# Score maxima in two parts: banks of their own for each, and moved steps, in pooled attention with two expert layers

## The chip, the cores and the metric

One Trainium2 chip, one of its cores. The metric is the device time of one execution in microseconds, median of the runs shown.

## The reference

```python
# attention: B=4, H=8, S=1152, D=64, query rows pooled in twos
q_pool = q.reshape(B, H, S // 2, 2, D).mean(axis=3)
scores = np.matmul(q_pool, k.transpose(0, 1, 3, 2)) / np.sqrt(D)
scores = scores - np.max(scores, axis=-1, keepdims=True)
attn = np.exp(scores)
attn = attn / (np.sum(attn, axis=-1, keepdims=True) + 1e-09)
x = np.matmul(attn, v)                    # then (2304, 512) = tokens x features
# soft mixture: logits over 32 slots, softmax over tokens (dispatch) and over slots (combine)
logits = x @ phi
d = softmax(logits, axis=0); slot_input = d.T @ x
slot_out[e] = np.maximum(slot_input[e] @ w1[e], 0) @ w2[e]     # 8 experts of 4 slots, width 1024
x = softmax(logits, axis=1) @ slot_out
# second layer: each token goes to its best expert by cosine with expert_emb / tau
out[mask] = gate_w[mask, None] * (np.maximum(x[mask] @ w1[e], 0) @ w2[e])
```

## The kernel before

All is float32. The work on the attention goes by pairs of heads: 16 pairs, four for each of the four batches, and 18 steps for each pair (`step`, L663; n counts all steps, i the pair, s the step in it). A step of pair i computes scores of one block of 128 keys against one half of the 576 pooled query rows, for the two heads: per head two matmuls into one bank (`scores`, L366; the second, L375, adds the low part of the query and, by a row of ones, the negated maximum) and an Exp on ScalarE into a `pt` tile (L376). Steps 0 to 8 are the first half of the queries, 9 to 17 the second. The weighted sums with V (`weighted`, L425) of a half are done at one go, at step 10 for the first and at step 1 of the next pair for the second (`VISITS`), 36 matmul instructions at L433; behind the second the sums of the weights go through matmuls with ones (`weight_sums`, L402, first at L410), whose input `acc` is added up by GpSimd (`add_up`, L379: L389, L391, L397) from `pt` and from a partial sum `part` by VectorE (L394, steps 9 and 18, which is step 0 of the next pair).

The maxima have to be known before the scores. For the pair ahead they are found in nine pieces (j = 0 to 8) of 64 query rows for each of two heads: `s_max` (L322) multiplies 128 rows with the 1152 keys, three matmuls of 384 columns into the three banks of a tile `s` (L334), and VectorE reduces the tile (L343) to one negated maximum a row, in column j of `nm`. There is one such tile (pool `ps_s`, one buffer of three banks; the other five banks are the ring `ps_e`, `new_e`, `new_t`). In the first pair some maxima are found "apart", in three banks of the ring, by three reductions and a joining one (L340, L341). `n_group` (L346) transposes `nm` for pieces 0 to 4 (`n0`, step 12) or 5 to 8 (`n1`, step 3 of the pair itself), and two small DMAs put it into `ql` (L354).

The order is written out by hand, in tables from step to action (L34 to L53): `MAXS` the pieces of the maximum, `SIDE` the other work on TensorE (q0, q1: transposing pooled queries; n0, n1; r: reciprocals of the sums; x0 to x2: normalised rows and logits), `FIRST` and `FMAX` the same for pair 0, `BATCH` the work at a batch's end. `keys_ahead` (L647) follows `TURN`, `HIGH` and `REST`: a third of the keys of pair i+2 is transposed by VectorE (L278), copied rounded by ScalarE (L281), and the remainder is formed by GpSimd (L285). Keys are loaded into one buffer `kn` by four DMAs at step 15 (`KLOAD`, L246, for pair i+3); `HEADS` says when a third of the keys is copied by head into `u` by DMAs from SP's queue (L291, L292), `LOADW` when a quarter of a weight tile is loaded (L588). In one step the order of issue is: scores, maximum, side work, batch work, weighted sums, the rests of side and batch work (on VectorE and ScalarE), `add_up` for the step before, `keys_ahead`, `q_by_heads`, `by_heads`, key load, query load, V load, weight piece. Every engine, and SP's queue of DMAs, takes its instructions in this order.

At a batch's end, in the second pair after it, `max_group` (L502; table value 18, so step 0) transposes the logits of 576 rows into the first bank of an `s` tile, VectorE takes the maximum over them (L508) and joins it with that of earlier batches (L510), and ScalarE's Exp reads the bank (L512). `d_group` (19, step 1) transposes the result, `sl_group` (21, step 3) multiplies it with the rows. The last batch's groups follow the loop (L714 on), and then the two expert layers, whose weights come from HBM by loads at L127.

Of the kernel before, what the change touches and what calls it, by code (L numbers as in the profile page):

```python
# [8 lines left out]
F32 = mybir.dt.float32  # L9
F32R = mybir.dt.float32r  # L10
I32 = mybir.dt.int32
AF = mybir.ActivationFunctionType
ALU = mybir.AluOpType
AX = mybir.AxisListType
PSUM = bass.MemoryType.PSUM
ET = mybir.EngineType
P = 128
# [14 lines left out]


SIDE = {5: 'q1', 7: 'r', 9: 'x0', 1: 'q0', 13: 'x2', 12: 'n0', 3: 'n1', 14: 'x1'}  # L34
MAXS = {2: 0, 4: 1, 6: 2, 8: 3, 10: 4, 16: 7, 1: 8, 14: 6, 11: 5}
BATCH = {18: 'm', 19: 'd', 21: 's'}

TURN = {2: 0, 9: 2, 12: 1}
FTURN = {9: 1, 11: 0, 10: 2}
HIGH = {16: 2, 13: 1, 11: 0}  # L40
REST = {17: 0, 8: 1, 10: 2}
HEADS = (11, 15, 17)
QHEADS = 6
VISITS = (10, 19)

# [2 lines left out]
FQHEADS = 14  # L48

PREAT = 2  # L50
LOADW = (3, 6, 10)
QLOAD, KLOAD, VLOAD, QSUM = 5, 15, 6, 12
FQLOAD, FQSUM = 12, 17  # L53

# [2 lines left out]
def kernel(  # L57
# [14 lines left out]
    nc = tc.nc  # L72
    B, H, S, D = q.shape
# [3 lines left out]
    J = PQ // 64  # L77
    JB = J // 2
    NPAIR = H // 2
    KC = S // 3  # L80
# [14 lines left out]
    ident = const.tile([P, P], F32, name="ident")  # L95
# [43 lines left out]
    apart = const.tile([P, P // NS, NS], F32, name="apart")  # L139
# [27 lines left out]
    smax = [keep.tile([P, 1], F32, name=f"smax{b}") for b in range(B)]  # L167
# [4 lines left out]
    sm = att.enter_context(tc.tile_pool(name="sm", bufs=4))  # L172
    xp = att.enter_context(tc.tile_pool(name="xp", bufs=1))
# [8 lines left out]
    pairs = [{"b": i // NPAIR, "hp": i % NPAIR} for i in range(NPT)]  # L182
    xb = [{} for _ in range(B)]
# [24 lines left out]
    kh = [khl.tile([P, S], F32R, name=f"kh{i}") for i in range(2)]  # L208
    qb = [khl.tile([P, n, P], F32R, name=f"qb{g}") for g, n in enumerate((6, J - 6))]
# [8 lines left out]
    ps_s = att.enter_context(tc.tile_pool(name="ps_s", bufs=1, space=PSUM))  # L218
# [50 lines left out]
    def new_e():  # L269
        return ps_e.tile([P, 512], F32, tag="e", name="e")  # L270

    def new_t():
        return new_e()


    def turn(i, g):
        t = pairs[i]["kl", g] = khl.tile([P, KC], F32R, tag=f"kl{g}", name=f"kl{g}", bufs=2)
        nc.vector.transpose(out=t.bitcast(F32), in_=pairs[i]["kn"][:, 12 * g : 12 * g + 12].rearrange("p n d -> p (n d)"))  # L278
# [8 lines left out]
    def by_heads(i, g):  # L287
        cs = slice(g * KC, (g + 1) * KC)
        for h in range(2):
            hi, lo = kh[i % 2][own[h], cs].bitcast(F32), pairs[i]["kl", g][own[h]].bitcast(F32)  # L290
            nc.sync.dma_start(out=uw[g][0:64, :, h].bitcast(F32), in_=hi.unsqueeze(1).to_broadcast([64, 2, KC]))  # L291
            nc.sync.dma_start(out=us[g][64:128, h].bitcast(F32), in_=lo)  # L292
# [21 lines left out]
    def q_by_heads(i, cs=None):  # L314
        _, qh, ql = sets[i % 2]
        cs = cs or slice(0, PQ)
        for h in range(2):
            for dst, src in ((qh[0:64], hq), (qh[64:128], hq), (ql[0:64], lq)):
                nc.sync.dma_start(out=dst[:, h, cs].bitcast(F32), in_=src[own[h], cs].bitcast(F32))


    def s_max(i, j, apart=False):  # L322
        p = pairs[i]
        if j in (0, 5):
            p["nm", j] = sm.tile([P, 5], F32, tag="nm", name="nm", bufs=3)
        j0 = 5 if j > 4 else 0
        nm = p["nm", j0][:, j - j0 : j - j0 + 1]
        if apart:
            ss = [new_e()[:, 0:KC] for _ in range(3)]
        else:  # L330
            s = ps_s.tile([P, 3, 512], F32, tag="s", name="s")
            ss = [s[:, c, 0:KC] for c in range(3)]
        for c in range(3):
            nc.tensor.matmul(  # L334
                ss[c], qb[j // 6][:, j % 6, :], kh[i % 2][:, c * KC : (c + 1) * KC], start=True, stop=True
            )
        if apart:
            n3 = sm.tile([P, 3], F32, tag="n3", name="n3", bufs=2)
            for c in range(3):
                nc.vector.tensor_reduce(out=n3[:, c : c + 1], in_=ss[c], axis=AX.X, op=ALU.max, negate=True)  # L340
            nc.vector.tensor_reduce(out=nm, in_=n3, axis=AX.X, op=ALU.min)  # L341
        else:
            nc.vector.tensor_reduce(out=nm, in_=s[:, :, 0:KC], axis=AX.XY, op=ALU.max, negate=True)  # L343


    def n_group(i, part):  # L346
        j0, n = (5, J - 5) if part else (0, 5)
        t = new_t()
        nc.tensor.transpose(t[0:n, 0:P], pairs[i]["nm", j0][:, 0:n], ident)
        nr = sm.tile([5, P], F32R, tag="nr", name="nr", bufs=2)  # L350
        nc.scalar.activation(out=nr[0:n], in_=t[0:n, 0:P], func=AF.Copy)
        ql = sets[i % 2][2]
        for h in range(2):
            nc.sync.dma_start(  # L354
                out=ql[64:65, h, j0 * 64 : (j0 + n) * 64].rearrange("o (j q) -> o j q", q=64).bitcast(F32),
                in_=nr[0:n, own[h]].bitcast(F32),
            )
        yield
# [141 lines left out]


    def max_group(b):  # L502
        t = ps_s.tile([P, 3, 512], F32, tag="s", name="s")[:, 0, :]
        nc.tensor.transpose(t[:, 0:P], lk[:, b * JB : (b + 1) * JB, :].rearrange("p m n -> p (m n)"), ident)
        n = P + 64
        nc.tensor.transpose(t[:, P:n], xb[b]["l4"].rearrange("p m n -> p (m n)"), ident[0:64, 0:64])
        yield
        nc.vector.tensor_reduce(out=smax[b], in_=t[:, 0:n], axis=AX.X, op=ALU.max, negate=True)  # L508
        if b:
            nc.vector.tensor_tensor(out=smax[b], in0=smax[b], in1=smax[b - 1], op=ALU.min)  # L510
        dt = xb[b]["dt"] = xp.tile([P, P + 64], F32, tag="dt", name="dt")
        nc.scalar.activation(out=dt, in_=t[:, 0 : P + 64], func=AF.Exp, bias=smax[b])  # L512
        if b:
            cor = xb[b]["cor"] = sm.tile([P, 1], F32, tag="cor", name="cor", bufs=1)
            nc.scalar.activation(out=cor, in_=smax[b - 1], func=AF.Exp, scale=-1.0, bias=smax[b])
# [27 lines left out]
    def slot_sums(b, t):  # L543
        x, xr, d = (xb[b][n] for n in ("x", "xr", "d"))
        for m in range(JB):
            ms = slice(m * NS, (m + 1) * NS)
            nc.tensor.matmul(t[ms], d[:, 0, ms], x[:, m, :], start=True, stop=False, tile_position=(0, m * NS))
        for m in range(JB):
            ms, cs = slice(m * NS, (m + 1) * NS), slice(m * P, (m + 1) * P)
            nc.tensor.matmul(t[ms, cs], d[0:64, 1, ms], xr[:, cs], start=False, stop=True, tile_position=(0, m * NS))  # L550

    def sl_group(b):
        t = ps_s.tile([P, 3, 512], F32, tag="s", name="s")[:, 0, :] if b == B - 1 else new_t()
        slot_sums(b, t)
        yield
        if b == B - 1:
            new = xb[b]["new"] = xp.tile([P, DM], F32, tag="new", name="new")
            nc.scalar.activation(out=new, in_=t, func=AF.Copy)
        elif b:
            nc.vector.scalar_tensor_tensor(  # L560
                out=slots, in0=slots, scalar=xb[b]["cor"], in1=t, op0=ALU.mult, op1=ALU.add
            )
        else:
            nc.vector.tensor_copy(slots, t)
# [60 lines left out]
    for h in range(2):  # L625
        nc.sync.dma_start(
            out=ip[own[h], :, P + h * NS : P + (h + 1) * NS], in_=phi.rearrange("(c p) n -> p c n", p=P)[own[h]]
# [5 lines left out]
    def begin(live, g):  # L633
        live.append(g)
        next(g, None)
# [11 lines left out]
    def keys_ahead(i, s):  # L647
        if i + 2 < NPT:
            if s in (TURN if i else FTURN):
                turn(i + 2, (TURN if i else FTURN)[s])  # L650
            if s in HIGH:
# [11 lines left out]
    def step(n):  # L663
        i, s = divmod(n, NCH)
        live = []
        if n < NST:
            for h in range(2):
                scores(n, h)
            early = i == 0
            if s in (FMAX if early else MAXS):  # L670
                j = (FMAX if early else MAXS)[s]
                at = i + 1 - (s < 6 and j > 4)
# [4 lines left out]
            for late in range(2):  # L677
                at, s1 = i - 1 - late, s + NCH * late
                if at > 0 and pairs[at]["hp"] == NPAIR - 1 and s1 in BATCH:
                    begin(live, {"m": max_group, "d": d_group, "s": sl_group}[BATCH[s1]](pairs[at]["b"]))  # L680
        for u in range(2):
# [10 lines left out]
        if n < NST:  # L692
            keys_ahead(i, s)
            if s == (QHEADS if i else FQHEADS) and i + 1 < NPT:
                q_by_heads(i + 1)
            if s in HEADS and i + 1 < NPT:
                by_heads(i + 1, HEADS.index(s))
            if s == KLOAD and i + 3 < NPT:
# [5 lines left out]
            if s == VLOAD and 1 < i + 1 < NPT:  # L704
                load_v(i + 1)
            if s in LOADW and i >= PREAT:
                load_w_part((i - PREAT) * len(LOADW) + LOADW.index(s))

    n = 0
# [5 lines left out]
    n, b = NPT - 1, B - 1  # L715
# [34 lines left out]
    ts = [new_e() for _ in range(4)]  # L750
# [233 lines left out]
    t = new_tr()  # L984
# [5 lines left out]
    t = new_tr()  # L990
# [35 lines left out]
    t = new_tr()  # L1026
# [236 lines left out]
```

## Time and profile before

| what | value |
|---|---|
| median of 3 runs | 701.2 us (697.88 to 702.91) |
| the profiled execution, its time | 700.93 us |
| its span, first to last instruction | 698.9 us |
| TensorE matmuls busy | 655.8 us (94%) |
| VectorE busy | 391.9 us (56%) |
| ScalarE busy | 341.7 us (49%) |
| GpSimd busy | 372.4 us (53%) |
| mean granted clock of TensorE | 0.975 of full speed |
| the chain that ended last, shares of the span | TensorE 73%, VectorE 8%, DMA 5%, ScalarE 3% |

PE is TensorE's matmuls, PEld its weight loads (they run ahead of the matmuls), DVE is VectorE, ACT ScalarE, POOL GpSimd, SPq the queue of DMAs that SyncE issues. Busy matmuls overlap, so a busy share of 94% does not mean that the array is at its peak. Times are microseconds from the span's start, unless a column says ns. The 2 us between span and time lie around the span.

### The profile page before, as it was taken

How to read it: one execution, taken by the hardware profiler on the slowest of the kernel's cores; microseconds unless marked ns; L12 is line 12 of the kernel's file. 1: busy time of each engine (PE TensorE's matmuls, PEld its weight loads, DVE VectorE, ACT ScalarE, POOL GpSimd, SP SyncE). 2: the span in 40 equal slices, each digit the busy share in tenths (PEclk: the TensorE clock that was granted, in tenths of full speed). 3: DMA queues.
4: the chain of work that ended last, by engine and by line, in shares of the span. 5: the costliest groups of instructions: out<-in, count | busy, mean ns of one | idle time of the engine just before them, and what ended most of it. 6: DMA issues, size and time to landing. Idle time of an engine off the chain costs nothing.

```text
span 698.9 us, 12442 instructions
## 1 busy us (share of the span) xinstructions
PE 655.8 (94%) x4330; PEld 495.7 (71%) x4330; DVE 391.9 (56%) x611; ACT 341.7 (49%) x944; POOL 372.4 (53%) x403
## 2 busy tenths in 40 slices
PE   5788999999999999999999999999988989999996
PEld 3655788777687778768778876877753366888885
DVE  5456667667676666767657676764344325522210
ACT  2245566555566556546555654645514046632221
POOL 5454788688777878867678886767700001000000
PEclk9579999999999999999999999999999999999999
DMA  7958778897778978858897895844899924031111
GB/s 135 179 88 177 164 142 215 156 202 198 128 191 165 205 194 150 206 102 214 157 188 189 153 216 92 215 110 106 297 349 385 354 88 155 18 73 46 46 45 48
DMA packets 185090, 114.28 MB, mean 164 GB/s; under 512 B 120888, under 2 KB 158520, under 8 KB 185024
## 3 DMA queue, kind: packets, MB, share of 16 engines
q1 hardware_dynamic: 182976, 112.46, 67.7%
q10 hardware_dynamic: 2048, 0.98, 0.8%
q8 instruction: 36, 0.59, 0.4%
q14 instruction: 30, 0.25, 0.1%
HBM read 66.14 MB, written 4.72 MB: 101 GB/s over the span
## 4 chain that ended last, share of the span: by engine, by line
PE 73%; DVE 8%; DMA 5%; ACT 3%; issue 2%; POOL 1%; SPq 0%; ACTq 0%; POOLq 0%
PE e L433 20%; PE h L1150 14%; PE s L334 11%; PE e L374 8%; PE e L375 7%; DVE nm L343 6%; PE e L469 3%; DMA w<-in_moe_w 2%; DMA en<-in_moe_expert_emb 2%; PE e L410 1%; ACT pt L376 1%; PE e L302 1%; PE h L868 1%; PE h L842 1%; DMA x<-in_moe_w 1%
## 5 line engine op out<-in xcount | busy, mean ns | idle before, releaser
L343 DVE TENSOR_REDUCE nm<-s 128x1 f32<-128x1152 f32 x142 | 192.1, 1353 | 120.1 <-PE s L334 120.0
L376 ACT ACTIVATE pt<-e 128x288 f32<-128x288 f32 x576 | 199.4, 413 | 63.7 <-PE e L375 55.5
L391 POOL TENSOR_TENSOR acc<-acc,pt 128x576 f32<-128x576 f32 x127 | 180.0, 1418 | 15.0 <-ACT pt L376 9.0
L374 PE MATMUL e<-qh,u 128*128 128x288 f32 x576 | 180.1, 328 | 1.2 <-ACT pt L376 1.2
L375 PE MATMUL e<-ql,u 65*128 65x288 f32 x576 | 165.2, 303 | 2.8 <-DMA ql<-nr 2.8
L433 PE MATMUL e<-pt,v 128*64 128x288 f32 x1152 | 149.7, 415 | 0.0
L334 PE MATMUL s<-kh,qb 128*128 128x384 f32 x426 | 109.4, 366 | 15.7 <-DVE nm L343 8.7
L433 PEld LDWEIGHTS e<-pt,v 128*64 128x64 f32 x1152 | 81.0, 139 | 59.6 <-ACT pt L376 5.4
L374 PEld LDWEIGHTS e<-qh,u 128*128 128x128 f32 x576 | 111.9, 194 | 13.6 <-issue 7.6
L375 PEld LDWEIGHTS e<-ql,u 65*128 65x128 f32 x576 | 112.0, 194 | 4.1 <-DMA u<-kh 2.2
L334 PEld LDWEIGHTS s<-kh,qb 128*128 128x128 f32 x426 | 72.1, 197 | 27.9 <-DVE nm L343 17.9
L435 ACT ACTIVATE xu<-e 128x288 f32<-128x288 f32 x32 | 13.1, 410 | 128.5 <-PE e L433 128.5
L389 POOL TENSOR_TENSOR acc<-pt 128x576 f32<-128x576 f32 x32 | 45.4, 1418 | 53.5 <-PE e L418 45.1
L394 DVE TENSOR_REDUCE part<-pt 128x576 f32<-128x1728 f32 x32 | 68.1, 2129 | 0.0
L397 POOL TENSOR_TENSOR acc<-acc,part 128x576 f32<-128x576 f32 x31 | 43.6, 1407 | 36.6 <-DVE part L394 36.5
L1150 PE MATMUL h<-xh,hh 128*128 128x512 f32 x144 | 57.5, 400 | 0.0
L1150 PE MATMUL h<-xh,hl 128*128 128x512 f32 x144 | 57.0, 396 | 0.0
L1150 PE MATMUL h<-xl,hh 128*128 128x512 f32 x144 | 57.0, 396 | 0.0
L285 POOL TENSOR_TENSOR kl<-kl,kh 128x384 fp32r<-128x384 f32 x48 | 48.0, 1001 | 0.6 <-ACT kh L281 0.6
L1127 POOL CAST xh<-x 128x512 fp32r<-128x512 f32 x6 | 3.4, 613 | 63.8 <-PE t L1110 63.8
L1142 DVE SCALAR_TENSOR_TENSOR hl<-c,hh 128x512 fp32r<-128x512 f32 (+1 forms) x22 | 14.0, 642 | 37.8 <-ACT hh L1141 37.8
L469 PE MATMUL e<-ip,xu 128*128 128x192 f32 x160 | 33.9, 328 | 0.0
(232 smaller groups left out, 686.5 us busy)
## 6 DMA issues: line engine op xcount, KB each, us to landing
w<-in_moe_w SPq DMA_DIRECT2D x23, 1024.0 KB
u<-kh SPq DMA_DIRECT2D x96, 192.0 KB
kn<-in_k SPq DMA_DIRECT2D x64, 144.0 KB
u<-kl SPq DMA_DIRECT2D x96, 96.0 KB
v<-in_v SPq DMA_DIRECT2D x32, 288.0 KB
w<-in_moe_w SPq DMA_DIRECT2D x36, 256.0 KB
qh<-hq SPq DMA_DIRECT2D x60, 144.0 KB
qr<-in_q SPq DMA_DIRECT2D x28, 160.0 KB
```

The costliest lines, as they stand in the source:

```text
L285: eng.tensor_tensor(out=t, in0=t.bitcast(F32), in1=hi, op=ALU.subtract)
L334: nc.tensor.matmul(ss[c], qb[j // 6][:, j % 6, :], kh[i % 2][:, c * KC : (c + 1) * KC], start=True, stop=True)
L343: nc.vector.tensor_reduce(out=nm, in_=s[:, :, 0:KC], axis=AX.XY, op=ALU.max, negate=True)
L374: nc.tensor.matmul(e, us[j // 3][:, h, ks], qh[:, h, qs], start=True, stop=False)
L375: nc.tensor.matmul(e, ws[j // 3][:, h, ks], ql[:, h, qs], start=False, stop=True)
L376: nc.scalar.activation(out=pt(n)[:, h, :], in_=e, func=AF.Exp, scale=1.0 / 16.0)
L389: eng.tensor_tensor(out=acc, in0=pt(n - 1), in1=pt(n), op=ALU.add)
L391: eng.tensor_tensor(out=acc, in0=acc, in1=pt(n), op=ALU.add)
L394: nc.vector.tensor_reduce(out=p["part"], in_=pts[n // 3].rearrange("p j h q -> p h q j"), axis=AX.X, op=ALU.add)
L433: nc.tensor.matmul(p["pv"][own[h], 0:HQ], vs[:, h, j, :], pt(n)[:, h, :], start=j == 0, stop=j == J - 1)
L469: nc.tensor.matmul(t[:, n * PW : (n + 1) * PW], xu[:, m * P : (m + 1) * P], ip[:, hp, :], start=True, stop=True)
L1150: nc.tensor.matmul(o, x[:, c, sl], y[:, c, :], start=c + r == 0, stop=c == FC - 1 and r == 2)
```

## The change

A maximum that isn't apart uses two tiles: `sa` of two banks for the first 768 keys and `sb` of one bank for the last 384, each with its own reduction, into two columns of `nm`, which is now five by two. At pieces 4 and 8 one more reduction joins the columns into `nn`, which `n_group` transposes. A maximum apart puts its three results into the two columns and `n1`, and a two-input minimum joins `n1`. `max_group` takes a bank of the ring, and ScalarE copies the 192 columns to SBUF at once; maximum and Exp work on the copy. In the tables: piece 3 goes from step 8 to 9; the batch's groups m and d go one step later; the first of the three key transpositions goes from step 2 to 0 (in pair 0 another from 9 to 8); the second group of head copies goes from step 15 to 16, behind the key load of step 15; one weight piece goes from step 3 to 1.

```diff
-MAXS = {2: 0, 4: 1, 6: 2, 8: 3, 10: 4, 16: 7, 1: 8, 14: 6, 11: 5}
-BATCH = {18: 'm', 19: 'd', 21: 's'}
-TURN = {2: 0, 9: 2, 12: 1}
-FTURN = {9: 1, 11: 0, 10: 2}
+MAXS = {2: 0, 4: 1, 6: 2, 10: 4, 16: 7, 1: 8, 14: 6, 11: 5, 9: 3}
+BATCH = {21: 's', 20: 'd', 19: 'm'}
+TURN = {9: 2, 12: 1, 0: 0}
+FTURN = {11: 0, 10: 2, 8: 1}
-HEADS = (11, 15, 17)
+HEADS = (11, 16, 17)
-LOADW = (3, 6, 10)
+LOADW = (1, 6, 10)
...
     def s_max(i, j, apart=False):
-            p["nm", j] = sm.tile([P, 5], F32, tag="nm", name="nm", bufs=3)
+            p["nm", j] = sm.tile([P, 5, 2], F32, tag="nm", name="nm", bufs=3)
...
         if apart:
-            ss = [new_e()[:, 0:KC] for _ in range(3)]
+            ts = [new_e() for _ in range(3)]
+            for c in range(3):
+                part(ts[c], c)
+            n1 = sm.tile([P, 1], F32, tag="n1", name="n1", bufs=2)
+            for t, n in zip(ts, (nm[:, 0:1], nm[:, 1:2], n1)):
+                nc.vector.tensor_reduce(out=n, in_=t[:, 0:KC], axis=AX.X, op=ALU.max, negate=True)
+            nc.vector.tensor_tensor(out=nm[:, 0:1], in0=nm[:, 0:1], in1=n1, op=ALU.min)
         else:
-            s = ps_s.tile([P, 3, 512], F32, tag="s", name="s")
-            ss = [s[:, c, 0:KC] for c in range(3)]
...
-            nc.vector.tensor_reduce(out=nm, in_=s[:, :, 0:KC], axis=AX.XY, op=ALU.max, negate=True)
+            s = ps_s.tile([P, 2, 512], F32, tag="sa", name="sa")
+            for c in range(2):
+                part(s[:, c], c)
+            nc.vector.tensor_reduce(out=nm[:, 0:1], in_=s[:, :, 0:KC], axis=AX.XY, op=ALU.max, negate=True)
+            s = ps_s.tile([P, 512], F32, tag="sb", name="sb")
+            part(s, 2)
+            nc.vector.tensor_reduce(out=nm[:, 1:2], in_=s[:, 0:KC], axis=AX.X, op=ALU.max, negate=True)
+        if j in (4, J - 1):
+            n = j - j0 + 1
+            nn = p["nn", j0] = sm.tile([P, 5], F32, tag="nn", name="nn", bufs=3)
+            nc.vector.tensor_reduce(out=nn[:, 0:n], in_=p["nm", j0][:, 0:n], axis=AX.X, op=ALU.min)
...
     def max_group(b):
-        t = ps_s.tile([P, 3, 512], F32, tag="s", name="s")[:, 0, :]
+        t = new_t()
...
+        dt = xb[b]["dt"] = xp.tile([P, n], F32, tag="dt", name="dt")
+        nc.scalar.activation(out=dt, in_=t[:, 0:n], func=AF.Copy)
         yield
-        nc.vector.tensor_reduce(out=smax[b], in_=t[:, 0:n], axis=AX.X, op=ALU.max, negate=True)
+        nc.vector.tensor_reduce(out=smax[b], in_=dt, axis=AX.X, op=ALU.max, negate=True)
...
-        dt = xb[b]["dt"] = xp.tile([P, P + 64], F32, tag="dt", name="dt")
-        nc.scalar.activation(out=dt, in_=t[:, 0 : P + 64], func=AF.Exp, bias=smax[b])
+        nc.scalar.activation(out=dt, in_=dt, func=AF.Exp, bias=smax[b])
...
     def sl_group(b):
-        t = ps_s.tile([P, 3, 512], F32, tag="s", name="s")[:, 0, :] if b == B - 1 else new_t()
+        t = ps_s.tile([P, 512], F32, tag="sb", name="sb") if b == B - 1 else new_t()
```

## Rows read from the trace of the kernel before

**Rows 1.** Chain that ended last: start us, us, what; weighted sums of step 1

```profile
122.35 4.52 PE e L433 x36
...
151.01 4.52 PE e L433 x36
...
422.25 6.01 PE e L433 x36
```

**Rows 2.** Who waited for whom, whole run: us in total, times, longest us

```profile
PEld s L334 <- DVE nm L343: 17.9, 35, 1.6
```

**Rows 3.** Timeline, steps 2, 4 and 8 of one pair: start, us, engine, line

```profile
156.78 0.68 PE L334 MATMUL s<-kh,qb 128*128 128x384 f32 x3
...
157.50 1.36 DVE L343 TENSOR_REDUCE nm<-s 128x1 f32<-128x1152 f32 x1 [3.89 <-PE s L334]
...
158.91 0.47 PEld L334 LDWEIGHTS s<-kh,qb 128*128 128x128 f32 x3 [0.51 <-DVE nm L343]
158.91 0.79 PE L334 MATMUL s<-kh,qb 128*128 128x384 f32 x3 [0.28 <-DVE nm L343]
...
163.41 0.48 PEld L334 LDWEIGHTS s<-kh,qb 128*128 128x128 f32 x3 [0.28 <-DVE nm L343]
```

**Rows 4.** VectorE's groups by shape: busy us, mean ns, idle before

```profile
L343 DVE TENSOR_REDUCE nm<-s 128x1 f32<-128x1152 f32 x142 | 192.1, 1353 | 120.1 <-PE s L334 120.0
...
L340 DVE TENSOR_REDUCE n<-e 128x1 f32<-128x384 f32 x6 | 3.0, 549 | 0.0
...
L341 DVE TENSOR_REDUCE nm<-n 128x1 f32<-128x3 f32 x2 | 0.3, 155 | 0.1
```

**Rows 5.** Timeline of TensorE, end of pair 0: first and last of six maxima

```profile
52.74 0.80 PE L334 MATMUL s<-kh,qb 128*128 128x384 f32 x3 [0.41 <-DVE nm L343]
...
63.97 0.79 PE L334 MATMUL s<-kh,qb 128*128 128x384 f32 x3
```

**Rows 6.** Timeline of GpSimd and VectorE at the second batch's maximum

```profile
295.50 2.88 POOL L391 TENSOR_TENSOR acc<-acc,pt 128x576 f32<-128x576 f32 x2
...
297.18 1.22 DVE L510 TENSOR_TENSOR smax<-smax,smax 128x1 f32<-128x1 f32 x1
```

**Rows 7.** Timeline of weight loads at the first and the second batch's maximum

```profile
178.59 0.14 PEld L504 LDWEIGHTS s<-ident,lk 128*128 128x128 f32 x1 [0.66 <-POOL lk L492]
...
180.02 0.47 PEld L334 LDWEIGHTS s<-kh,qb 128*128 128x128 f32 x3 [0.41 <-ACT dt L512]
...
298.96 0.82 PEld L334 LDWEIGHTS s<-kh,qb 128*128 128x128 f32 x3 [1.72 <-ACT dt L512]
```

**Rows 8.** Stretch in the third batch's weighted sums: engines' busy us, clock, DMA

```profile
423.50:425.00 1.50, 1.50 (x8) 0.70 (x6) 0.52 (x2) 0.00 (x0) 0.31 (x1) 0.50 1.10 244
```

**Rows 9.** Timeline: Exp of the last batch, and SP's first loads behind `nr`

```profile
514.66 0.42 ACT L512 ACTIVATE dt<-s,smax 128x192 f32<-128x192 f32 x1 [5.31 <-DVE smax L510]
...
490.45 26.56 SPq L127 DMA_DIRECT2D w<-in_moe_w  x12
```

**Rows 10.** Timeline of SP's queue and VectorE around two key loads

```profile
147.18 0.69 SPq L291 DMA_DIRECT2D u<-kh  x1
...
149.97 4.15 SPq L246 DMA_DIRECT2D kn<-in_k  x4
...
149.75 2.13 DVE L394 TENSOR_REDUCE part<-pt 128x576 f32<-128x1728 f32 x1
...
158.78 0.57 DVE L278 STREAM_TRANSPOSE kl<-kn 128x384 f32<-128x384 f32 x1
...
39.38 2.83 SPq L246 DMA_DIRECT2D kn<-in_k  x4
...
46.48 0.58 DVE L278 STREAM_TRANSPOSE kl<-kn 128x384 f32<-128x384 f32 x1 [1.90 <-DMA kn<-in_k]
```

**Rows 11.** Timeline at step 1: GpSimd's last addition, sums of weights

```profile
152.89 1.43 POOL L397 TENSOR_TENSOR acc<-acc,part 128x576 f32<-128x576 f32 x1
...
155.46 0.16 PEld L410 LDWEIGHTS e<-acc,ones 128*32 128x32 f32 x8 [0.44 <-issue]
```

More of the change, by code (lines that the diff above doesn't have):

```diff
@@ L324, in s_max, with part @@
         if j in (0, 5):
-            p["nm", j] = sm.tile([P, 5], F32, tag="nm", name="nm", bufs=3)
+            p["nm", j] = sm.tile([P, 5, 2], F32, tag="nm", name="nm", bufs=3)
         j0 = 5 if j > 4 else 0
-        nm = p["nm", j0][:, j - j0 : j - j0 + 1]
-        if apart:
-            ss = [new_e()[:, 0:KC] for _ in range(3)]
-        else:
-            s = ps_s.tile([P, 3, 512], F32, tag="s", name="s")
-            ss = [s[:, c, 0:KC] for c in range(3)]
-        for c in range(3):
+        nm = p["nm", j0][:, j - j0]
+        def part(t, c):
             nc.tensor.matmul(
-                ss[c], qb[j // 6][:, j % 6, :], kh[i % 2][:, c * KC : (c + 1) * KC], start=True, stop=True
+                t[:, 0:KC], qb[j // 6][:, j % 6, :], kh[i % 2][:, c * KC : (c + 1) * KC], start=True, stop=True
             )
         if apart:
-            n3 = sm.tile([P, 3], F32, tag="n3", name="n3", bufs=2)
+            ts = [new_e() for _ in range(3)]
             for c in range(3):
-                nc.vector.tensor_reduce(out=n3[:, c : c + 1], in_=ss[c], axis=AX.X, op=ALU.max, negate=True)
-            nc.vector.tensor_reduce(out=nm, in_=n3, axis=AX.X, op=ALU.min)
-        else:
-            nc.vector.tensor_reduce(out=nm, in_=s[:, :, 0:KC], axis=AX.XY, op=ALU.max, negate=True)
+                part(ts[c], c)
[3 more added lines that the diff above has]
+            nc.vector.tensor_tensor(out=nm[:, 0:1], in0=nm[:, 0:1], in1=n1, op=ALU.min)
+        else:
+            s = ps_s.tile([P, 2, 512], F32, tag="sa", name="sa")
[9 more added lines that the diff above has]
+            nc.vector.tensor_reduce(out=nn[:, 0:n], in_=p["nm", j0][:, 0:n], axis=AX.X, op=ALU.min)
     def n_group(i, part):
@@ L348, in n_group @@
         t = new_t()
-        nc.tensor.transpose(t[0:n, 0:P], pairs[i]["nm", j0][:, 0:n], ident)
+        nc.tensor.transpose(t[0:n, 0:P], pairs[i]["nn", j0][:, 0:n], ident)
         nr = sm.tile([5, P], F32R, tag="nr", name="nr", bufs=2)
```

## The prediction, made before the change was run

> **What bounds the kernel now.** I read the chain of waits first, for the period of one head pair, then who waits for whom, then one pair in the timeline, then the groups by shape. The chain is TensorE's over most of the span. From the weighted sums at 122.35 us to the same piece one pair later it takes 28.66 us [rows 1], and a pair without a batch's work on top takes about that. In that period TensorE is short of work only where a score maximum has to wait: all three banks of `s` go to VectorE as one tile, one reduction reads them, and the matmuls of the next maximum may not write until it has ended. Over the run TensorE's weight loads wait 17.9 us for it [rows 2]. In one pair: step 2's matmuls (0.68 us) are followed by a reduction of 1.36 us from 157.50, and step 4's first load waits 0.51 us for its end [rows 3]. The other wait of that pair, 0.28 us, is at step 8 [rows 3], so 0.8 us a pair are shown as idle. After a wait the pipeline has to fill again: three matmuls then take 0.79 us in place of 0.68 [rows 3], at three places (steps 4, 6 and 8). That makes 0.8 + 3 x 0.11 = 1.13 us a pair.
>
> **The split.** A reduction of 1152 columns takes 1353 ns and one of 384 takes 549 ns [rows 4]. The slope is 804 ns / 768 = 1.047 ns a column, so 768 columns cost 147 + 804 = 951 ns. The pair costs 951 + 549 = 1.50 us, 0.15 us more than the one; run directly behind each other VectorE's instructions overlap by some 0.08 us, so +0.07 to +0.15 us for each of 142 maxima, 10 to 21 us of VectorE time in all. VectorE is busy 56% of the span and stands idle 120.1 us in front of these reductions [rows 4], which covers it. The 31 new joining reductions over five by two numbers are priced by the reduction over 128x3, 155 ns [rows 4]; one ends far ahead of the transposition that reads it (steps 10 to 12 and 1 to 3 have a visit of 4.5 us of weighted sums between), so I count nothing for it, at most 0.15 us a time.
>
> What is gained is the release. Two banks are free 0.95 us after their matmuls, not 1.36, and the third bank's matmul and the whole second reduction lie beside the next work. A cycle of maximum upon maximum was reduction plus fill, 1.36 + 0.80 + 0.09 = 2.25 us; it becomes 0.95 + 0.69 = 1.64 us, and over two steps TensorE's own work then lasts longer, so these waits go. Per pair I take 0.95 us, between the 0.8 shown idle and the 1.13 with the fill. From pair 1's second half to that of pair 14 there are 14 such periods: **13.3 us** (11.2 to 15.8). With j=3 moved from step 8 to step 9 the three maxima at 9, 10 and 11 stand close, but behind that of step 10 TensorE has its 4.5 us of weighted sums.
>
> **Pairs 0 and 1.** There a maximum stands in nearly each step, and six starts lie 2.25 us apart, (63.97 - 52.74) / 5 [rows 5], where TensorE has 1.0 to 1.7 us of work. With a cycle of 1.64, 0.6 us go at each of five gaps: 3.0 us, and half a microsecond for the like waits at the start of pair 0: **3.5 us** (2 to 4.5). The first five maxima, before the first scores, are bound by VectorE itself; 0.3 to 0.5 us more work there stand against a start half a microsecond earlier (two of three matmuls suffice): nothing, within 0.5 us either way.
>
> The Trainium skill (SBUF — State Buffer, "SBUF: two separate sides") has a rule against one edit here: a VectorE operation with two SBUF inputs and a GpSimd operation that reads SBUF lock each other out for the whole instruction. The trace agrees: a 128x1 minimum took 1.22 us and ended at 298.40, when GpSimd's two sums ended at 298.38 [rows 6]. The new minimum in a maximum taken apart is such an operation, where a reduction stood; by the rule two of them could cost up to 2 us, and the sum would be 683. I don't count it, since GpSimd has short operations there.
>
> **The logits of a batch.** Three batches pass inside the loop. Their transpositions now wait 0.66 us for GpSimd's sum, then the next maximum waits for Exp to let the tile go: 0.41 us in the first, 1.72 us in the next two [rows 7]. The long idle time lowers the granted clock: 0.50 from 423.50 to 425.00 [rows 8], the lower of the two levels (1.2 GHz), and those weighted sums take 6.01 us, not 4.52 [rows 1]. So 1.1, about 3.4 and 3.9 us can go, 8.4 us. One step later the sums are ready and the bank is freed by a copy. But the transposition of the result, at step 2, then waits for a longer row of work: the copy, VectorE's queue, the two-input minimum (up to 1.22 us, [rows 6]), Exp. I take 0.7 us each (0 to 1.5): **6.3 us** net (3.9 to 8.4). In the last batch nothing lies beside it: a copy as long as the Exp, 0.42 us [rows 9], comes onto the path: **-0.5 us**.
>
> **The moved steps.** The key load moves ahead of one group of head copies in SP's queue (that group goes from step 15 to 16), so its four DMAs are issued where the copies are now, at 147.18 in place of 149.97 [rows 10]. The first transposition of these keys moves from step 2 to step 0, from 158.78 to right behind the reduction of 149.75, about 151.9 [rows 10]. It is a new wait: behind it on VectorE stand j=8's two reductions, the q remainder and the batch's maximum, and TensorE's steps 2 and 3 need their banks. How long a key load takes the trace bounds: under 8.8 us from the first issue (no wait at 158.78), and 7.1 us where it was waited for (39.38 to 46.48) [rows 10]. At 7.1 the keys are there at 154.3; 0.57 + 1.43 + 0.15 + 0.55 us later, at 157.0, all is done (0.55 us for the remainder is an estimate, after the reduction over as many columns), and step 3 needs its bank right behind step 2's maximum, whose first matmul is at 156.78 [rows 3], so at some 157.1. It just fits, with 0.1 us over. The copies that now come behind the key load are issued 3 to 4 us later, and are wanted at step 3 also. The weight piece at step 1, not 3, stands behind the copies and ahead of the small `nr` copies; these are wanted six steps later. For all of this, and for GpSimd below, I take **-0.15 us** a pair, 2.1 us (0 to 7). In pair 0 the transposition at step 8 waits for keys that came at 46.48, and the sum of weights behind it starts 4 us later; GpSimd has idled over 5 us there.
>
> The sum: 13.3 + 3.5 + 6.3 - 0.5 - 2.1 = 20.5 us. What follows the attention shifts with it, as SP starts the weight loads behind the last `nr` copy, at 490.45 [rows 9]. The profiled execution took 700.93 us, 0.27 under the median of 701.2; 701.2 - 20.5 is **681 us**. The likeliest case by its own bounds: 28.2 us at best, 673; at worst 11.2 + 2 + 3.9 - 0.5 - 7 = 9.6, 692.
>
> **Rivals.** *The keys come too late* (the slower side). From 7.2 us after the first issue on, each further microsecond stops TensorE at steps 2 and 3 of 13 pairs: 13 us for one. At 8.7 the gain is used up, at 9.5 the run takes some 711 us. For it: the 7.1 us leave 0.1. Against it: under 8.8 is known, and copies no longer run ahead of the load. Chance 0.08.
>
> *GpSimd's chain takes the place.* The sums of weights after each pair wait for its last addition, which ends at 154.32 (152.89 + 1.43); TensorE gets there at 155.46 [rows 11]. From the partial sum of step 9 on GpSimd runs without a gap, and that partial sum now stands behind a maximum's two reductions: 0.7 us later against TensorE. 0.4 us are left. If it is 2 us later, 0.9 us a pair come back, 12.6 us: 693. Chance 0.12.
>
> *The split doesn't free the banks early*, as the third matmul stands in TensorE's queue behind the second reduction: the cycle is 1.43 + 0.69 = 2.1 us, 0.15 less than now. Then about 4 us come from the maxima and 6 from the batches: 691. Against it: that bank's matmul is third in line, 0.3 us behind the first. Chance 0.05.
>
> **How the numbers follow.** The forecast has 0.75. A change under 1%, 7 us, can hardly be told from none. The likeliest case and most of GpSimd's and the split's are faster by more, so 0.83; within 1% 0.10, from the tops of these and the keys about 8.7 us under way; slower 0.07, the late keys. The range is 670 to 696.
>
> **What would show it.** Right: a period of 27.5 to 27.9 us; loads of the maxima waiting for VectorE well under 5 us in the run; reductions of 0.95 and 0.5 us; weighted sums of 4.5 us in each batch; no granted clock of 0.5 between 60 and 480 us. Wrong: idle time before the key transposition or TensorE waiting for the q remainder (the keys); the 128x256 sums of ones waiting for GpSimd (its chain); a maximum's first load still waiting over 0.3 us (the split).

## The result, and the profile after

The changed kernel takes 681.02 us (median of 4 runs, 678.84 to 681.38), the kernel before beside it 700.62 us (697.88 to 702.91). The ratio of the runs on record is 0.9688, 95% interval 0.9645 to 0.9732; the quotient of the two medians, 0.9720, lies within it. The profiled execution took 680.75 us, with a span of 678.6.

The page of the changed kernel: the busy line, and the shares of the chain that ended last.

```profile
PE 644.8 (95%) x4330; PEld 491.4 (72%) x4330; DVE 404.0 (60%) x785; ACT 339.6 (50%) x948; POOL 372.5 (55%) x403
...
PE 81%; DMA 7%; DVE 2%; ACT 1%; POOL 1%; issue 1%; SPq 0%; ACTq 0%; POOLq 0%
```

VectorE works 12.1 us more than before and has 2% of the chain instead of 8%: the change pays VectorE time, which was to spare, for waits of TensorE. DMA has gone from 5% to 7%: another wait has taken a part of the place, as the chain below shows. Groups by line, engine and operation, which answer to [rows 4] (busy us, mean ns | idle before them):

```profile
L346 DVE TENSOR_REDUCE nm<-sa 128x1 f32<-128x768 f32 x142 | 134.7, 949 | 84.8 <-PE sa L330 84.8
L349 DVE TENSOR_REDUCE nm<-sb 128x1 f32<-128x384 f32 x142 | 77.5, 546 | 0.0
L278 DVE STREAM_TRANSPOSE kl<-kn 128x384 f32<-128x384 f32 x48 | 27.0, 569 | 20.7 <-DMA kn<-in_k 20.5 <-DMA qr<-in_q 0.2
```

Who waits for whom (us in total, times, longest), to set against [rows 2]:

```profile
DVE kl L278 <- DMA kn<-in_k: 20.5, 14, 5.6
...
PEld e L385 <- DMA ql<-nr: 7.0, 5, 4.0
...
PEld sa L330 <- DVE nm L346: 3.6, 5, 1.1
```

The maxima's loads wait 3.6 us in 5 places, where it was 17.9 in 35. All five lie before 60 us, in pair 0 and ahead of it; from pair 1 on no first load of a maximum waits for a reduction. In one pair, steps 2 and 4 (timeline; [rows 3] has the kernel before):

```profile
155.75 0.96 DVE L346 TENSOR_REDUCE nm<-sa 128x1 f32<-128x768 f32 x1 [0.68 <-PE sa L330]
156.62 0.55 DVE L349 TENSOR_REDUCE nm<-sb 128x1 f32<-128x384 f32 x1
156.76 0.32 PEld L330 LDWEIGHTS sa<-kh,qb 128*128 128x128 f32 x2
```

The next maximum's first load comes at 156.76, when the first reduction (155.75 + 0.96 = 156.71) has just let go of its two banks and the second has 0.41 us still to run. That is the whole idea of the split in three lines.

The chain, weighted sums at step 1 of a pair (L443; first in pair 1, then pair 2 and so on), against [rows 1]:

```profile
65.05 5.50 PE e L443 x36
...
93.71 4.51 PE e L443 x36
...
121.38 4.52 PE e L443 x36
...
149.43 4.52 PE e L443 x36
...
206.95 4.52 PE e L443 x36
...
262.83 4.52 PE e L443 x36
...
320.51 4.51 PE e L443 x36
...
377.40 4.52 PE e L443 x36
...
434.95 4.52 PE e L443 x36
...
462.51 4.52 PE e L443 x36
```

The same visits of pairs 2 and 15 in the kernel before:

```profile
93.71 4.52 PE e L433 x36
...
481.88 4.52 PE e L433 x36
```

One reads four things here. Up to 93.71 nothing is gained: before, that visit stood at 93.71 too. From there to the visit of pair 15 it takes 368.80 us where it was 388.17 (93.71 to 481.88), 19.37 us less, nearly the whole gain. Of the seven pairs without a batch in this stretch three take 27.6 to 27.7 us (as 93.71 to 121.38), four 28.05 to 28.65; in those four the chain runs over a DMA, twice the row of maxima (`ql`), twice the copies of key halves (`u`). One of each:

```profile
144.02 3.27 DMA ql<-nr
...
256.28 4.52 DMA u<-kl
```

And the three stretches of two pairs with a batch in them take 57.52, 57.68 and 57.55 us (149.43 to 206.95, 262.83 to 320.51, 377.40 to 434.95), where they took 60.00, 63.05 and 63.09. All sums take some 4.5 us now but the first, whose clock the windows show (the number ahead of the DMA share and GB/s):

```profile
62.00:64.00 2.00, 1.87 (x10) 1.66 (x11) 1.46 (x1) 1.33 (x4) 0.46 (x1) 0.90 0.80 128
64.00:66.00 2.00, 2.00 (x10) 1.09 (x10) 0.00 (x0) 1.00 (x3) 0.95 (x1) 0.50 1.07 168
```

From 62 to 480 us this is the only place where windows of 2 us show 0.5 (1.2 GHz); before there were two, behind the second and third batch.

### The profile page after: what moved, and what is told of

Its sections match the earlier page's. It is cut to its first block, busy times and chain, and to the rows that moved or that the text cites. A ratio compares the mean times of both kernels' runs of the same rounds, so it can differ in the third digit from the quotient of the medians.

```text
span 678.6 us, 12632 instructions
## 1 busy us (share of the span) xinstructions
PE 644.8 (95%) x4330; PEld 491.4 (72%) x4330; DVE 404.0 (60%) x785; ACT 339.6 (50%) x948; POOL 372.5 (55%) x403
## 4 chain that ended last, share of the span: by engine, by line
PE 81%; DMA 7%; DVE 2%; ACT 1%; POOL 1%; issue 1%; SPq 0%; ACTq 0%; POOLq 0%
PE e L443 20%; PE h L1162 15%; PE e L384 11%; PE e L385 10%; PE sa L330 6%; PE sb L330 3%; PE e L479 3%; DMA w<-in_moe_w 2%; DMA en<-in_moe_expert_emb 2%; DMA ql<-nr 1%; PE e L302 1%; PE e L420 1%; DMA u<-kl 1%; PE t L1122 1%; PE h L880 1%; PE h L854 1%
## 5 line engine op out<-in xcount | busy, mean ns | idle before, releaser
L386 ACT ACTIVATE pt<-e 128x288 f32<-128x288 f32 x576 | 196.2, 413 | 56.9 <-PE e L385 47.7
L346 DVE TENSOR_REDUCE nm<-sa 128x1 f32<-128x768 f32 x142 | 134.7, 949 | 84.8 <-PE sa L330 84.8
L443 PE MATMUL e<-pt,v 128*64 128x288 f32 x1152 | 149.1, 414 | 0.0
L443 PEld LDWEIGHTS e<-pt,v 128*64 128x64 f32 x1152 | 80.7, 139 | 57.9 <-ACT pt L386 4.3
L330 PE MATMUL sa<-kh,qb 128*128 128x384 f32 x284 | 76.5, 350 | 4.1 <-DVE nm L346 2.2
L349 DVE TENSOR_REDUCE nm<-sb 128x1 f32<-128x384 f32 x142 | 77.5, 546 | 0.0
L399 POOL TENSOR_TENSOR acc<-pt 128x576 f32<-128x576 f32 x32 | 45.5, 1421 | 44.6 <-PE e L428 36.1
L330 PEld LDWEIGHTS sa<-kh,qb 128*128 128x128 f32 x284 | 47.4, 196 | 6.9 <-DVE nm L346 3.6
L330 PE MATMUL sb<-kh,qb 128*128 128x384 f32 x142 | 51.6, 364 | 0.0
L278 DVE STREAM_TRANSPOSE kl<-kn 128x384 f32<-128x384 f32 x48 | 27.0, 569 | 20.7 <-DMA kn<-in_k 20.5
```

The source lines that it names most:

```text
L330: nc.tensor.matmul(t[:, 0:KC], qb[j // 6][:, j % 6, :], kh[i % 2][:, c * KC : (c + 1) * KC], start=True, stop=True)
L346: nc.vector.tensor_reduce(out=nm[:, 0:1], in_=s[:, :, 0:KC], axis=AX.XY, op=ALU.max, negate=True)
L349: nc.vector.tensor_reduce(out=nm[:, 1:2], in_=s[:, 0:KC], axis=AX.X, op=ALU.max, negate=True)
L386: nc.scalar.activation(out=pt(n)[:, h, :], in_=e, func=AF.Exp, scale=1.0 / 16.0)
L399: eng.tensor_tensor(out=acc, in0=pt(n - 1), in1=pt(n), op=ALU.add)
L443: nc.tensor.matmul(p["pv"][own[h], 0:HQ], vs[:, h, j, :], pt(n)[:, h, :], start=j == 0, stop=j == J - 1)
```

## Experiments: the split

Each run's "steady part" below is the time on its chain from the step-1 visit of pair 2 to that of pair 15, 13 pairs: 388.17 us before, 368.80 in the changed kernel. The kernel before, timed beside each of these runs, took 701.5 to 703.1 us (medians); ratios are to that. Visits are of one profiled execution each.

**Split alone.** The tables, and `max_group` with its Exp on the bank (in the first bank of `sa`), as before:

```diff
-MAXS = {..., 9: 3}   BATCH = {21: 's', 20: 'd', 19: 'm'}   TURN = {9: 2, 12: 1, 0: 0}
+MAXS = {..., 8: 3}   BATCH = {18: 'm', 19: 'd', 21: 's'}   TURN = {2: 0, 9: 2, 12: 1}
-FTURN = {..., 8: 1}  HEADS = (11, 16, 17)  LOADW = (1, 6, 10)
+FTURN = {9: 1, ...}  HEADS = (11, 15, 17)  LOADW = (3, 6, 10)
...
-        t = new_t()
+        t = ps_s.tile([P, 2, 512], F32, tag="sa", name="sa")[:, 0, :]
```

> The two-part maxima of the changed kernel, with the step tables of the kernel before and a batch's logits read from their bank twice (in the first tile of the maxima), as before. Theory (the first part's banks come free early, which takes the VectorE wait out of the period; the batch cost is another thing): periods without a batch near 27.8 us instead of 28.65, so some 14 x 0.85 = 12 us off, the three batches keep most of their some 9 us: 688 to 691 us. Rival 1 (the moved steps make the gain): 698 to 702 us. Rival 2 (the batch cost too came from the single tile of the maxima): 680 to 684 us.

Measured: 687.61 us (686.76 to 691.26), ratio 0.9813 (0.9754 to 0.9871), just under the 688 to 691 expected.

```profile
91.23 4.51 PE e L443 x36
...
468.26 4.52 PE e L443 x36
```

Its steady part is 377.03 us, 11.14 less than before; four of the seven pairs without a batch take 27.6 to 27.7 us (as 91.23 to 118.92), three 28.25 to 28.73, and those with a batch keep all of their price: 60.63, 61.69 and 58.66 us for two pairs. So the split gives 13 us by the ratio, 14.6 by the medians, of the 19.6.

**Moves alone.** All tables and the copied logits of the changed kernel, the maxima as before:

```diff
-            s = ps_s.tile([P, 2, 512], F32, tag="sa", name="sa")
+            s = ps_s.tile([P, 3, 512], F32, tag="s", name="s")
...
-            nc.vector.tensor_reduce(out=nm[:, 0:1], in_=s[:, :, 0:KC], axis=AX.XY, op=ALU.max, negate=True)
...
+            nc.vector.tensor_reduce(out=nm, in_=s[:, :, 0:KC], axis=AX.XY, op=ALU.max, negate=True)
```

> The changed kernel with the maxima in one tile of three banks and one reduction, as before; moved steps and the copied logits stay. Theory: periods without a batch stay at 28.6 us with loads of maxima waiting for the reduction (some 15 us in all), the batches give up some 9 us: 690 to 694 us. Rival 1 (moved steps make the gain): 680 to 684 us. If the moves cost what the prediction put down for them (2.1 us) and the batches give only its 6.3: 696 to 698 us.

Measured: 697.34 us (696.05 to 698.39), ratio 0.9928 (0.9901 to 0.9955): the third expectation, not the first.

```profile
95.76 4.51 PE e L433 x36
...
477.70 4.52 PE e L433 x36
```

A pair takes 28.84 us (95.76 to 124.60), 0.2 more than before, and the batches cost less (59.55, 60.63, 59.93). Between this run and the changed kernel only the split differs: 381.94 - 368.80 = 13.14 us in the steady part, and 2.05 us up to its start (95.76 against 93.71).

**One tile, two reductions.** The split's instructions without its banks: one tile of three banks, let go after both.

```diff
-            s = ps_s.tile([P, 2, 512], F32, tag="sa", name="sa")
-            for c in range(2):
+            s = ps_s.tile([P, 3, 512], F32, tag="s", name="s")
+            for c in range(3):
                 part(s[:, c], c)
...
+            nc.vector.tensor_reduce(out=nm[:, 1:2], in_=s[:, 2, 0:KC], axis=AX.X, op=ALU.max, negate=True)
```

> The changed kernel, but the three column blocks of a maximum share one tile again, released after both reductions; two instructions and moved steps stay. Theory (what counts is that two banks come free after the first reduction): as the run with one reduction, plus up to 0.14 us a maximum where it is waited for: 690 to 697 us, loads of maxima waiting for VectorE 15 to 20 us in all. Rival (two short instructions are as good as separate banks): 680 to 684 us.

Measured: 702.57 us (701.66 to 704.1), ratio 1.0019 (0.9994 to 1.0044), above the 690 to 697 expected.

```profile
93.83 4.52 PE e L441 x36
...
482.50 4.52 PE e L441 x36
```

A pair takes 29.45 us (123.28 to 152.73), and the steady part 388.67. The groups of TensorE at the maxima:

```profile
L330 PE MATMUL s<-kh,qb 128*128 128x384 f32 x426 | 108.3, 363 | 21.4 <-DVE nm L347 19.0 <-ACT qb L306 1.9 <-ACT kh L281 0.2
...
L330 PEld LDWEIGHTS s<-kh,qb 128*128 128x128 f32 x426 | 71.5, 196 | 37.1 <-PE e L383 26.9 <-issue 3.8 <-POOL qr L259 1.9
```

The matmuls wait 19.0 us for the second reduction (the 26.9 us of the loads are put down to the matmul before, which had long been done: a wait for several things). So the second instruction by itself, with the joining reductions, costs 5.2 us (702.57 against 697.34), and its separate tile is worth 388.67 - 368.80 = 19.9 us in the steady part: that is shown by taking only the separate tile away. It does two things, which were not tried apart. The first reduction starts 0.55 us after the maximum's first matmul (155.20 to 155.75 in the changed kernel) and not 0.72 (129.05 to 129.77 here), while the third matmul still runs. And the banks come free behind that reduction, 0.96 us, not behind both, 1.43. Of 0.64 us a maximum, 0.17 are the earlier start and 0.47 the earlier release.

## Experiments: the batches and the moved steps

**Batch as before.** Only `max_group`'s tile and Exp, and `BATCH`, as in the first diff above.

> The changed kernel, but a batch's logits are read from their bank twice (in the first tile of the maxima) and the batch's three steps stand at 18, 19 and 21, as before. Theory (each of the three batches costs some 3 us by holding a tile of the maxima and by a slow weighted sum): 687 to 691 us, with a granted clock of 0.5 again in the windows behind the batches. Rival (the batch gain was the shorter period counted twice): 680 to 683 us.

Measured: 684.24 us (683.56 to 687.11), ratio 0.9755 (0.9698 to 0.9812). The two-pair stretches take 58.55, 58.99 and 59.02 us, together 3.8 more than in the changed kernel, and no window behind a batch has a clock of 0.5. The run is 3.2 us slower than the changed kernel; 6 to 10 were expected. Why does the same edit cost these 3.8 us here and more in the split alone? The second batch there, in the timeline (VectorE, GpSimd, TensorE; what ended the idle time in brackets):

```profile
290.34 2.89 POOL L401 TENSOR_TENSOR acc<-acc,pt 128x576 f32<-128x576 f32 x2
...
292.20 1.05 DVE L520 TENSOR_TENSOR smax<-smax,smax 128x1 f32<-128x1 f32 x1
...
293.82 0.30 PEld L330 LDWEIGHTS sa<-kh,qb 128*128 128x128 f32 x2 [1.55 <-ACT dt L522]
```

The 128x1 minimum lasts 1.05 us and ends at 293.25, GpSimd's two sums at 293.23; TensorE waits 1.55 us for the Exp behind it, and windows of 2 us from 294 on show a clock of 0.56 and 0.58. In the run of this section the same minimum started at 290.77, within the first of the two sums (289.71 to 292.62), and took 0.37 us. In the changed kernel it is one step later, at 295.58, in a gap of GpSimd (from 294.59 to 296.56):

```profile
L523 DVE TENSOR_TENSOR smax<-smax,smax 128x1 f32<-128x1 f32 x3 | 0.5, 159 | 0.1
```

The kernel before had 0.867 us in the mean for it:

```profile
L510 DVE TENSOR_TENSOR smax<-smax,smax 128x1 f32<-128x1 f32 x3 | 2.6, 867 | 0.1
```

When this two-input VectorE instruction starts within one of GpSimd's additions, it ends with that addition in these traces (293.25 and 293.23 above). The traces agree with the Trainium skill's rule (SBUF — State Buffer, "SBUF: two separate sides"): a VectorE operation with two SBUF inputs and a GpSimd operation that reads SBUF share a lock, and the one that starts second is blocked for the whole of the first.

Where a tile of the maxima is held until the Exp, a longer minimum went with a dearer batch: over two pairs of 27.7 us the second and the third batch cost 6.3 and 3.3 us in the split alone (minimum 1.05 and 0.29 us) and 3.6 us each here (0.37 us each). With the copy and the batch's steps one later it no longer does: in the run with both key steps put back, below, the minimum takes 0.68 and 0.63 us, and these batches cost no more than with 0.16. So the copy and the later steps together take the minimum off TensorE's path; which of the two does it was not tried.

**Key halves back to step 15**, all else as changed.

```diff
-HEADS = (11, 16, 17)
+HEADS = (11, 15, 17)
```

> The changed kernel with one moved step put back: the second group of key halves is copied in step 15, as before, instead of 16. Theory (the run with the split alone waited in a batch's pair for the row of the next maxima at 173.66 us, 0.73 us, behind such copies on SP's queue, and had a clock of 0.5 after it; that is where the moved steps pay some 4 us): 683 to 686 us. Rival (other moved steps make that gain, and this one only costs in pair 0): 678 to 681 us.

Measured: 695.01 us (693.89 to 698.16), ratio 0.9913 (0.9880 to 0.9945). Far more than expected, and for another reason: with the copies ahead of it the key load is issued later, while the transposition at step 0 still stands in VectorE's queue.

```profile
DVE kl L278 <- DMA kn<-in_k: 52.5, 13, 4.8
```

VectorE waits 52.5 us for keys instead of 20.5, in 13 pairs 2.5 us more each, and the steady part is 381.88 us, 13.08 longer: 1.0 us a pair. This is the rival of the late keys, at full size: the load had to move ahead for the transposition to move.

**Both put back.**

```diff
-TURN = {9: 2, 12: 1, 0: 0}   HEADS = (11, 16, 17)
+TURN = {9: 2, 12: 1, 2: 0}   HEADS = (11, 15, 17)
```

> The changed kernel with two moved steps put back together: the key halves are copied in step 15 and the first third of the keys is transposed in step 2, as before. Theory (the two belong together: copies behind the key load are what the early transposition needs, and the transposition alone is worth nothing): keys issued later, but wanted two steps later too, so not the 14 us of the copies alone; 681 to 683 us. Rival 1 (the key copies in step 16 are where the moved steps gain in the batches): 683.5 to 686 us. Rival 2 (in step 15 they still bring the keys too late): 690 to 695 us.

Measured: 679.98 us (678.01 to 682.12), ratio 0.9680 (0.9637 to 0.9723): as the changed kernel. VectorE waits for keys 6.1 us at one place, and the times show no gain from it; the steady part is 367.44 us, 1.4 shorter, in one execution. The minimum at its second batch starts within an addition of GpSimd:

```profile
291.49 1.41 POOL L407 TENSOR_TENSOR acc<-acc,part 128x576 f32<-128x576 f32 x1
...
292.24 0.68 DVE L523 TENSOR_TENSOR smax<-smax,smax 128x1 f32<-128x1 f32 x1
```

They end at 292.90 and 292.92. The stretches with the second and the third batch take 57.54 and 57.58 us all the same (261.11 to 318.65, 374.67 to 432.25; changed kernel 57.68 and 57.55).

**Transposition alone back to step 2**, the key halves in step 16.

```diff
-TURN = {9: 2, 12: 1, 0: 0}
+TURN = {9: 2, 12: 1, 2: 0}
```

> The changed kernel with one moved step put back: the first third of the next keys is transposed in step 2, as before, instead of step 0. VectorE then waits for those keys less (20.5 us in all now). Theory (with the key halves copied in step 16 the load is early enough, and the waits lie where nothing else is due): 680 to 682 us. Rival 1 (the moved transposition is what made the batches shorter): 683 to 685 us. Rival 2 (the waits for keys delay maxima now): 676 to 679 us.

Measured: 681.05 us (678.46 to 682.43), ratio 0.9706 (0.9643 to 0.9769). Its waits for keys are down to 4.3 us at one place. The 20.5 us that VectorE stands idle for keys in the changed kernel cost nothing that the times show; the steady part is 367.70 us, 1.1 shorter, in one execution.

**Fourth maximum back to step 8.**

```diff
-MAXS = {..., 9: 3}
+MAXS = {..., 8: 3}
```

> The changed kernel with one moved step put back: the fourth maximum is in step 8, as before, instead of step 9. Theory (of the three moved steps in which the run with the split alone and the run with the old batch steps differ, some 5 us in the steady part, this one and the keys' are left): 683 to 686 us. Rival (the keys' order on SP's queue makes all of it): 680 to 682 us.

Measured: 680.34 us (678.51 to 682.69), ratio 0.9700 (0.9636 to 0.9764). No difference again, and not the 683 to 686 expected. So the moved steps that I put back, one by one or as the pair of the keys, gain nothing beside the new batch steps; the key halves alone in step 15 cost 14 us, as their load then comes late. The split alone still loses 5.3 us in the steady part to the run with the old batch steps (377.03 against 371.75), which differ by those moves, one weight piece and one step of pair 0; in its first batch TensorE waited 0.40 us for key halves and 0.73 us for the row of maxima (172.77, 173.66), in the second for the slow minimum. Which moved step sets these two was not tried, and stays open.

## Experiments: why pairs 0 and 1 gave nothing

In the changed kernel the maxima of pair 0 are done sooner: the transposition of the second part (L359) is at 31.00 us, before at 35.45. Some of this is there before any bank is waited for: the first matmul of the first maximum stands at 9.58, before at 11.02. From it to the finished row for `ql`, when ScalarE's copy (L361) ends, it takes 24.16 us (to 33.74) where it was 26.88 (to 37.90), with the granted clock at 0.99 to 1.00 from 26 to 32 us, where it was 0.50. Then little comes of it: the row is issued at 36.74, before at 37.92, right when it was ready. SP's queue in the timeline:

```profile
34.00 1.34 SPq L638 DMA_DIRECT2D ip<-in_moe_phi  x2
35.39 1.25 SPq L265 DMA_DIRECT2D v<-in_v  x2
36.74 1.61 SPq L364 DMA_DIRECT2D ql<-nr  x2
...
53.00 2.63 SPq L234 DMA_DIRECT2D qr<-in_q  x4
...
59.98 1.53 SPq L364 DMA_DIRECT2D ql<-nr  x2
```

and TensorE in the same stretch (the first wait is put down to keys; its weight load, 4.05 us at 40.85, names the row):

```profile
40.86 0.61 PE L385 MATMUL e<-ql,u 65*128 65x288 f32 x1 [3.62 <-DMA kn<-in_k]
...
62.04 0.40 PE L385 MATMUL e<-ql,u 65*128 65x288 f32 x1 [1.66 <-DMA ql<-nr]
```

The row, two DMAs of 1.0 KB, stands 3 us behind phi and the values of pair 1, which nobody needs yet; at the end of the pair that of pair 1's first part, ready at 57.96, stands behind four loads of queries and the copies of `qh` and `ql`. Four runs test this.

**phi and V later**: both behind the key load of step 6.

```diff
-    for h in range(2):
-        nc.sync.dma_start(out=ip[own[h], ...], in_=phi...)
-    load_v(1)
...
         if i == 0 and s == 6:
             load_qk(2, "k")
             rest(1, 0, nc.gpsimd)
+            for h in range(2):
+                nc.sync.dma_start(out=ip[own[h], ...], in_=phi...)
+            load_v(1)
```

> The changed kernel; the loads of phi and of pair 1's v are issued in step 6 of pair 0 instead of before the loop, behind the row of pair 0's second part of maxima. Theory (SP's queue in order holds that row from 33.74 to 36.74 us and TensorE waits for it until 40.86): the row lands some 2.7 us earlier and everything behind it: 678 to 679 us. Rival (the wait that ends at 40.86 is for something else, or the gain is given back at the end of pair 0, where the maxima bound): 680.5 to 681.5 us.

Measured: 676.64 us (676.18 to 677.16), ratio 0.9635 (0.9598 to 0.9672), the fastest kernel with a small spread, and under the 678 to 679 expected. It is 4.4 us under the changed one, whose runs (678.84 to 681.38) it doesn't touch, nor those of the three kernels as fast as that (678.01 to 682.69). The two were not timed side by side, and the intervals of their ratios overlap a little.

```profile
34.05 1.33 SPq L364 DMA_DIRECT2D ql<-nr  x2
35.48 3.11 SPq L246 DMA_DIRECT2D kn<-in_k  x4
38.68 2.23 SPq L670 DMA_DIRECT2D ip<-in_moe_phi  x2
```

The row is issued 2.69 us earlier, and the wait of 3.62 us is gone: TensorE has work in every window of 2 us from 36 to 44 us, and its granted clock, which was 0.50 from 34 to 46 us, is at 1.00 from 40 to 56. That goes with 4.4 us, not 2.7; 4.27 of them stand at the step-1 visit of pair 2 (89.44 against 93.71).

**Pair 2's queries later**, at step 15.

```diff
-FQLOAD, FQSUM = 12, 17
+FQLOAD, FQSUM = 15, 17
```

> The changed kernel; in pair 0 the load of pair 2's q is issued in step 15 instead of 12, behind the row that carries pair 1's first maxima to the scores. Theory (at the end of pair 0 TensorE waits for that row, ready at 57.96 us but issued only at 59.98 behind four q loads and six copies on SP's queue, and the idle lowers the clock of the weighted sums at 65.05): row issued some 2 us earlier, that wait gone, 4.52 us instead of 5.50 for those sums: 678 to 680 us. Rival (VectorE's maxima bound the end of pair 0, or the later q comes too late for GpSimd's sum): 681 us or more.

Measured: 686.42 us (682.14 to 689.13), ratio 0.9776 (0.9731 to 0.9820): slower than the changed kernel, as the rival had it.

```profile
PE e L302 <- POOL qr L259: 6.5, 1, 6.5
```

TensorE waits 6.5 us for GpSimd's sum over the late queries. **Both**:

> The changed kernel with both loads later. Theory (SP's order bounds both places of pair 0): the sum of the two, 676 to 678 us. Rival (one of them is given back at the other): as the better of the two.

Measured: 682.50 us (679.46 to 686.07), ratio 0.9718 (0.9675 to 0.9762), again with that wait (7.1 us), and neither the 676 to 678 expected nor the better of the two. The queries have no slack there, phi and V have.

**Queries from ScalarE's queue**, with phi and V later; the queries stay at step 12.

```diff
-                load_qk(i + 2, "q")
+                load_qk(i + 2, "q", nc.sync if i else nc.scalar)
```

> The run with phi and pair 1's v issued later, and also pair 0's load of pair 2's q issued from ScalarE's queue at its old step 12. Theory (at the end of pair 0 SP's queue still holds the row of pair 1's maxima some 1.6 us behind its copy, TensorE waits 1.15 us and the clock falls for the sums that last 6.08 us): 674 to 676 us. Rival (2.6 us of issuing on ScalarE delay the exponentials there by as much): 676.5 to 679 us.

Measured: 676.62 us (672.14 to 678.0), ratio 0.9629 (0.9577 to 0.9681). In the profiled execution the row's delay at the end of pair 0 is gone (the chain's first step-1 visit):

```profile
58.78 4.52 PE e L443 x36
```

at 58.78 with 4.52 us, where the run with phi and V later has it at 60.27 with 6.08; yet the median is the same, within the rival's range, with a wide spread. Whether it is worth something is not settled.

## Why the prediction was right, and where its steps were not

The time was met, 681.0 against 681.02. The split, the main term, came about as forecast. That the time fits to 0.02 us is luck: the runs spread over 2.5 us, and other terms missed in both directions.

- *13.3 us for the split in 14 periods of 0.95*: 13.14 us in 13 pairs, 1.01 each, between the run with the moves alone and the changed kernel. A pair free of other waits takes 27.67 us against 28.84, which is 1.17, a little above my upper bound of 1.13; four of the seven without a batch give some of it back to the wait for the row of maxima (from 121.38 to 149.43 it takes 28.05) or for key halves (28.20 from 234.63). That these waits take the place of the old one is missing in the prediction. Most signs of being right came: 3.6 us of waiting loads, reductions of 0.95 and 0.55 us, sums of 4.5 us in each batch, and 27.5 to 27.9 us in three of those seven pairs. One didn't: the clock was 0.50 at 64 us. Two signs of being wrong came too, and meant less than was said: VectorE idled 20.5 us for keys, at no cost that the times show, and five loads of maxima waited 0.46 to 1.13 us, all by the end of pair 0. The joining reductions are 32, not 31, of 0.16 us each.
- *3.5 us in pairs 0 and 1*: failed. The profiled execution shows 0 up to 93.71. The cycle did fall, though less: two starts in pair 0 at 54.18 and 55.85 are 1.67 us apart, forecast 1.64, but the five gaps from 50.28 to 59.34 are 1.81 in the mean. Split against no split gives 2.05 us up to the visit of pair 2 (95.76 against 93.71), and the moves without the split lose as much; then SP's queue decides. The executions of other runs with the same pair 0 have that visit at 91.17, 91.82 and 92.76, so a single one can't tell 0 from 2.5. My step looked at TensorE and VectorE and counted five gaps; it never asked when the row that carries the maxima is issued.
- *6.3 us for three batches*: undersized, first in their price, taken as 1.1, 3.4 and 3.9 us. (Of the 3.4 for the second, the waits of 0.66 and 1.72 and sums of 5.04 us, 0.52 longer, account for 2.9.) Over two periods of 28.66 and 27.67 us they cost 14.2 us before (2.7, 5.7 and 5.8) and 6.7 now (2.2, 2.3 and 2.2): 7.5 us less. The 0.7 us a batch that I took off for the wait of d's transposition did not come: the minimum ends at 295.74, a microsecond before ScalarE comes to its Exp at 296.75. Even 0.68 us for it cost nothing (the run with both steps put back).
- *-0.5 us for the tail*: can't be told. From the visit of pair 15 to the end of the span it takes 216.1 us, before 217.0; over the runs here this goes from 215.9 to 218.9.
- *-2.1 us for the moved steps*: with the old maxima a pair takes 0.18 us more (28.84 against 28.66), as taken; beside the split the key steps put back shorten the steady part by 1.1 and 1.4 us in one execution each, and the medians by nothing that shows. What I had right is the order that bears it: "the key load moves ahead of one group of head copies", without which the runs show 14 us lost.
- *The key load*: issued at 145.66, the transposition starts at 152.51, 6.85 us later (7.1 taken). It just fits, as said: 3.7 us later in the run with the copies ahead, and each pair pays 1.0 us.
- *Rivals*: GpSimd's chain did not show: GpSimd waits there for TensorE, 36.1 us in the run, not TensorE for it. Banks not freed early: excluded by the three lines of the timeline. The rule of the Trainium skill on two SBUF inputs (SBUF — State Buffer, "SBUF: two separate sides") took nothing at the first maxima (both minima lasted 0.16 us).

## What to carry over

Ask of an accumulation tile not how long its reader takes, but when the first bank that the next writer needs comes free; two instructions on an engine with idle time may be longer in sum and still be worth 13 us in the steady part, 16 in the medians (697.34 against 681.02). When an engine's wait goes, follow the result to its next carrier, here a transfer of some 1 KB in an ordered queue behind loads that nobody needed yet. Moved steps come in pairs: a consumer may go ahead only as far as its load does.

## What was unexpected

A 128x1 minimum between two SBUF operands took from 0.16 to 1.22 us, by what GpSimd was doing at its start, and where a tile of the maxima was held for it, a longer one went with a dearer batch; behind the copied logits, one step later, 0.16 and 0.68 us cost the same. Twenty microseconds of VectorE waiting for keys cost nothing that the times show, 52 cost 13. And a row issued 2.7 us sooner gave 4.4 us, where the granted clock had stood at 0.50 around the wait for it.
